# Sine in the place of the angles, a tile of its own for VectorE's turning from slab 4 on, and new numbers for the planned order

## The chip, the cores and the metric

The kernel runs on one core of a Trainium2 chip. The metric is device time in microseconds (us) of one execution. Names of engines: PE is TensorE (matmuls and transposes), VectorE and ScalarE are the two vector engines that work beside it, GpSimd does next to nothing here, and SP issues the DMAs. Each engine works through its own list of instructions in order; semaphores hold an instruction until what it reads is there.

## The reference

The kernel computes a linear attention with a complex decay, and after it a gated feed-forward network. Everything is 32-bit float at the edge, except the three weight matrices, whose 64-bit words the kernel turns into 32-bit floats itself.

```python
mag = np.sqrt(a_re * a_re + a_im * a_im)
scale = np.minimum(mag, 0.999) / (mag + 1e-06)
a_re_n, a_im_n = a_re * scale, a_im * scale
for t in range(S):                       # 768 steps; B=4, H=8, D=48
    new_re = ar * S_re - ai * S_im
    new_im = ar * S_im + ai * S_re
    kv = np.einsum('bhd,bhe->bhde', k[:, :, t], v[:, :, t])
    S_re, S_im = new_re + kv, new_im
    y[:, :, t] = np.einsum('bhd,bhde->bhe', q[:, :, t], S_re)
...
g = x @ w_gate                           # 3072 tokens, 384 -> 1536
silu = g * (1.0 / (1.0 + np.exp(-g)))
out = (silu * (x @ w_val)) @ w_out       # 1536 -> 384
```

## The kernel before, in words

**Slabs and groups.** The 4 x 768 time steps are cut into 24 slabs of 128 steps with all 8 heads, and two slabs (two batches, the same stretch of time) make a group; there are 12 groups, numbered 0 to 11. Within a slab the attention is a masked product of keys and queries, plus a state `G` that is handed from one stretch of time to the next. The complex decay is taken out beforehand: keys and queries are scaled by the exponentials of cumulated logarithms and turned by the cosine and sine of cumulated angles, which doubles their 48 columns per head to 96.

**Staging a group** (`stage_ops`, planned for two slabs at a time, for group 0 for one slab each). Loads of the decay's real and imaginary part (tiles `re` and `im`), their squares (L366), the logarithm, and by a triangular matmul (L438) its cumulated sum; two exponentials (L453, L454); products of keys and queries with them (`kt`, `qt`); the arc tangent of the ratio, written to `im`; its cumulated sum (L441); the sum is reduced to a fraction of a turn in the tile called `s` (slot `s3`). Of that fraction the last row is sent to DRAM (the step `fr`), since the next stretch of time adds to it. Then ScalarE takes the absolute value, the cosine into `u`, and the sine over the fraction itself, in `s`. That last write must wait until `fr` has read the row. Four products make `ks` and `qs` of these (the step `turn`: twice with `u`, twice with `s`). Many tiles share a place: slot `s3`, for instance, also holds the logarithm of the next group, and slot `im` the next group's loaded `im`, so a place that is held longer makes the next group's load or logarithm start later.

**A slab's attention** (`slab_ops`). Keys and queries are transposed to a tile `T` with the 96 columns on the partitions. There are two ways. For the first slabs (before: slabs 0 to 5) PE does it, in four batches of four 128 x 96 transposes (L565) into a bank `p_gv`, and ScalarE or VectorE copies each batch to `T`. For the others VectorE transposes blocks of 32 x 32 (L585, two instructions for a slab) into a tile that is free once the weights have been split (`spare("w")`, named `ww`), and 12 DMAs on SP's queue move the blocks to their places in `T`. Then come the scores (L614, PE), the mask (L620, VectorE), the output product `av` (L645, PE), its copy to `xh` (L654, ScalarE) and the rounding rest `xl` (L661, VectorE), and the state's product `kv` (L672, PE) with its additions to `G`.

**The network** (`ffn_ops`) takes a group's `xh` and `xl` in 12 steps (g,f), f from 0 to 11: `f1` (L825, 18 matmuls, 12 in group 0) into a bank `p_gv`, of which there are two; the silu (L831, ScalarE); the product (L836, VectorE); the rounding to `hh` and the rest `hl` (L291); `f2` (L859, 6 matmuls, 4 in group 0) into `p_po`. `f1` of a group begins when `xh` and `xl` of both of its slabs are there.

**Weights.** VectorE turns each block's 64-bit words into floats in three steps (L724, L728, L732), group 0 uses them whole, and afterwards each block is split into two rounded halves (a cast, then a subtraction) that all later groups use. `range_ops` reads each weight block once more by a DMA into a tile `wo` and tests its range with one VectorE (L777) and one ScalarE instruction (L782); these 36 tests lie in the stretch behind group 0.

**What sets the order.** A planner (class `Planner`) is given every step by name, with the engines that may run it and a cost for each, its dependencies, and the slots that it takes or uses. It hands out the steps one after the other by due time, and the instructions are then written to each engine's list in that order. Due times of the network and the attention come from the anchors `T0`, `PER`, `FT`, `FT0`, `LEAD0`, `LEAD2`, `AHEAD`; those of the weights from `CONV0`, `CONVP`; those of the tests from `CK0`, `CKP`; other steps take theirs from what follows them. Where two engines may do a step, the planner chooses. Where ScalarE needs another function table, an ACT_TABLE_LOAD (L942) stands in its list.

## Time and profile before

| what | us |
|---|---|
| median of 3 runs (lowest to highest) | 661.78 (660.48 to 664.44) |
| the profiled execution | 661.93 |
| its span, first to last instruction | 660.2 |
| PE busy / VectorE busy / ScalarE busy | 626.5 / 500.6 / 398.5 |

What is not in the span, 661.93 - 660.2 = 1.73 us, lies around it. The page gives each engine's busy time and, by line, what its instructions cost and what they waited for; a window counts what each engine did in a stretch of the span; a row of the timeline is one instruction or some alike: its start, its duration, and in square brackets how long the engine had stood idle and what ended that. Successive matmuls overlap, so what one costs on PE is read from one start to the next.

### The profile page before, as it was taken

What the parts mean: (1) busy time and instruction counts of PE and PEld (TensorE: products, weight loads), DVE (VectorE), ACT (ScalarE), POOL (GpSimd) and SP (SyncE); (2) the same over time, 40 slices, a digit from 0 to 9 for tenths busy, and PEclk for the clock granted to TensorE, in tenths of its full rate; (3) what the DMA queues carried; (4) which work ended last, traced back from release to release, by engine and by line L of the source; (5) the groups of instructions that cost most, each with busy time, mean ns of one, the idle gap of its engine ahead of it and who ended that gap; (6) DMA issues with size and microseconds to landing.
All of it is one profiled execution on the core that took longest, in us unless ns stands there. A gap on an engine that the chain in (4) does not pass through costs nothing.

```text
span 660.2 us, 15503 instructions
## 1 busy us (share of the span) xinstructions
PE 626.5 (95%) x6306; PEld 586.9 (89%) x6306; DVE 500.6 (76%) x923; ACT 398.5 (60%) x654; POOL 3.0 (0%) x9
## 2 busy tenths in 40 slices
PE   2689999999998999999999999999999999999996
PEld 0367778899998998999999999999999999999996
DVE  8799999989877876976976976967876966643332
ACT  7855259876875866756956766967846836311110
POOL 1000000000000000000000000000000000000000
PEclk9999999999999899999999999999999999999999
DMA  9999502346745646655755656655543530320000
GB/s 190 302 296 288 134 25 62 65 92 124 163 104 121 168 110 130 155 135 120 159 128 125 150 130 131 138 132 118 122 104 65 125 85 12 75 57 1 25 1 29
DMA packets 234932, 77.49 MB, mean 117 GB/s; under 512 B 208859, under 2 KB 230621, under 8 KB 234854
## 3 DMA queue, kind: packets, MB, share of 16 engines
q1 hardware_dynamic: 234854, 76.43, 48.8%
q8 instruction: 51, 0.84, 0.6%
q14 instruction: 27, 0.22, 0.1%
HBM read 57.47 MB, written 4.78 MB: 94 GB/s over the span
## 4 chain that ended last, share of the span: by engine, by line
PE 65%; DVE 18%; DMA 7%; ACT 6%; issue 3%; SPq 0%; ACTq 0%; DVEq 0%
PE p_gv L825 34%; PE p_po L859 17%; PE p_ps L614 5%; PE p_py L645 5%; ACT L942 2%; DVE xl L728 2%; ACT s L346 2%; PE p_pm L672 1%; PE p_pm L441 1%; DMA wo<-in_moe_w_val_dram 1%; DVE sg L836 1%; DMA kt<-in_k_dram 1%; DMA wo<-in_moe_w_gate_dram 1%; DVE s L291 1%; DVE ks L291 1%
## 5 line engine op out<-in xcount | busy, mean ns | idle before, releaser
L825 PE MATMUL p_gv<-xh,ww 128*128 128x256 f32 x1596 | 316.8, 294 | 1.2 <-DVE sg L836 1.1
L825 PEld LDWEIGHTS p_gv<-xh,ww 128*128 128x128 f32 x1596 | 260.0, 190 | 9.0 <-DVE sg L836 2.5
L825 PE MATMUL p_gv<-xl,ww 128*128 128x256 f32 x726 | 204.6, 282 | 0.0
L942 ACT ACT_TABLE_LOAD x111 | 142.4, 1283 | 2.0
L831 ACT ACTIVATE sg<-p_gv 128x256 f32<-128x256 f32 x144 | 54.2, 383 | 140.4 <-PE p_gv L825 139.6
L825 PEld LDWEIGHTS p_gv<-xl,ww 128*128 128x128 f32 x726 | 137.6, 190 | 0.2 <-issue 0.2
L859 PE MATMUL p_po<-wo,hh 128*128 128x384 f32 x484 | 126.7, 343 | 0.0
L836 DVE TENSOR_TENSOR sg<-sg,p_gv 128x256 f32<-128x256 f32 x144 | 58.6, 413 | 63.9 <-ACT sg L831 63.9
L859 PEld LDWEIGHTS p_po<-wo,hh 128*128 128x128 f32 x484 | 82.0, 189 | 2.3 <-issue 2.2
L859 PE MATMUL p_po<-wo,hl 128*128 128x384 f32 x242 | 81.4, 336 | 0.0
L291 DVE TENSOR_TENSOR hl<-sg,hh 128x256 fp32r<-128x256 f32 x132 | 54.3, 418 | 7.0 <-ACT hh L295 1.7
L614 PE MATMUL p_ps<-T 96*128 96x128 f32 x384 | 53.2, 279 | 0.0
L614 PEld LDWEIGHTS p_ps<-T 96*128 96x128 f32 x384 | 50.7, 196 | 0.9 <-ACT T L295 0.3
L859 PEld LDWEIGHTS p_po<-wo,hl 128*128 128x128 f32 x242 | 45.4, 188 | 0.0
L295 ACT CAST hh<-sg 128x256 fp32r<-128x256 f32 x49 | 19.7, 403 | 34.5 <-DVE sg L836 29.4
L346 ACT ACTIVATE s<-s 128x768 f32<-128x768 f32 x44 | 36.7, 842 | 4.0 <-DVE s L291 3.5
L645 PE MATMUL p_py<-sc,vt 128*32 128x128 f32 x768 | 37.1, 273 | 1.2 <-ACT xh L654 0.7
L777 DVE TENSOR_REDUCE flags<-wo 128x1 f32<-128x384 f32 x36 | 19.7, 547 | 24.4 <-DMA wo<-in_moe_w_val_dram 11.1
L620 DVE TENSOR_TENSOR sc<-p_ps,tri 128x512 f32<-128x512 f32 x48 | 32.8, 682 | 4.0 <-PE p_ps L614 3.4
L645 PE MATMUL p_py<-T,G 96*32 96x128 f32 x640 | 33.5, 280 | 0.0
L825 PE MATMUL p_gv<-xh,ww-1_412 128*128 128x256 f32 x132 | 27.4, 297 | 1.6 <-ACT xh L654 1.6
L782 ACT ACTIVATE wo<-wo 128x384 f32<-128x384 f32 x36 | 20.2, 561 | 12.3 <-DMA wo<-in_moe_w_gate_dram 5.4
(134 smaller groups left out, 804.5 us busy)
## 6 DMA issues: line engine op xcount, KB each, us to landing
T<-ww SPq DMA_DIRECT2D x216, 64.0 KB, 2.1
wo<-in_moe_w_out_dram SPq DMA_DIRECT2D x24, 384.0 KB, 5.6
ww<-in_moe_w_gate_dram SPq DMA_DIRECT2D x12, 384.0 KB, 5.1
vt<-in_v_dram SPq DMA_DIRECT2D x24, 192.0 KB, 4.0
ww<-in_moe_w_val_dram SPq DMA_DIRECT2D x12, 384.0 KB, 6.2
out_dram<-ost SPq DMA_DIRECT2D x24, 192.0 KB, 2.3
wo<-in_moe_w_gate_dram SPq DMA_DIRECT2D x12, 384.0 KB, 3.4
wo<-in_moe_w_val_dram SPq DMA_DIRECT2D x12, 384.0 KB, 4.0
```

The costliest lines, as they stand in the source:

```text
L291: V[e].tensor_tensor(out=out, in0=a, in1=b, op=op)
L295: nc.scalar.copy(out=out, in_=in_)
L346: nc.scalar.activation(out=of(dst), in_=of(source), func=func, scale=scale, **kw)
L614: nc.tensor.matmul(out=ps[:, hh, :], lhsT=kT(4 * qd + hh), rhs=qT(4 * qd + hh), start=True, stop=True)
L620: nc.vector.tensor_tensor(out=s, in0=at_["ps", f"{n}.{qd}"].rearrange("p (h t) -> p h t", h=4), in1=mask.unsqueeze(1).to_broadcast([P, 4, ...
L645: nc.tensor.matmul(out=o, lhsT=l, rhs=r, start=opens, stop=closes, tile_position=(0, 32 * slot))
L782: nc.scalar.activation(out=high(0), in_=high(1), func=AF.Square, accum_out=flags[:, fl_hi + j:fl_hi + j + 1])
L825: nc.tensor.matmul(out=gv[:, i, :], lhsT=l, rhs=r, start=(m == 0), stop=(m == len(mm) - 1))
L831: nc.scalar.activation(out=new("sg", I), in_=at_["gv", I][:, 0:2 * P], func=AF.Silu)
L836: nc.vector.tensor_tensor(out=sg, in0=sg, in1=at_["gv", I][:, 2 * P:4 * P], op=ALU.mult)
L859: nc.tensor.matmul(out=po, lhsT=l[:, cs], rhs=weight("o", f, part), start=f == 0 and j == 0, stop=f == NF - 1 and j == len(products) - 1)
L942: nc.scalar.preload_act_table_set(op.load)
```

## The change

Four things are edited. The sine is written to the place of `im`, which is no longer needed by then, instead of over the fraction; the dependency on `fr` is dropped, and `im` stays held until the products with the sine are made. The limit between the two ways of transposing goes from slab 6 to slab 4 (`TURN`). VectorE's way now has a tile of its own (`turned`, slot `bt`) instead of the spare weight tile, so that it no longer waits for the weights' split or for the end of group 0. To make room for that tile the scratch space for dynamic DMAs is set to 8192. And the costs, the anchors and other numbers that the planner goes by are replaced, which moves instructions everywhere.

```diff
--- before.py
+++ after.py
@@ -29,20 +29,20 @@
 INV_2PI = 0.15915494309189535
 LN999_2 = 2.0 * math.log(0.999)
 
-SWITCH = 1.527
-HOP = 0.189
-SWITCH_KEY = 8.8
-STRETCH = 1.749
-AHEAD, YIELD, QUEUED = -15.32, 14.38, 5.384
-T0, PER, FT, FT0 = 47.32, 23.02, 3.999, 5.679
-LEAD0, LEAD2 = 8.605, 2.123
-CONV0, CONVP = 39.06, 28.89
+SWITCH = 1.216
+HOP = 0.155
+SWITCH_KEY = 8.525
+STRETCH = 0.957
+AHEAD, YIELD, QUEUED = 14.73, 14.3, 3.586
+T0, PER, FT, FT0 = 50.04, 22.62, 3.712, 3.252
+LEAD0, LEAD2 = 13.23, 3.651
+CONV0, CONVP = 36.84, 13.29
 T1 = T0 + 12 * FT0
-CK0, CKP = 167.9, 18.96
-RCP, SQR = 1, 2
+CK0, CKP = 171.5, 11.84
+RCP, SQR, TURN = 1, 2, 4
 HIGH, LOW, WHOLE = 0, 1, 2
-SHY = -9.417
-POOL_FROM = 9.827
+SHY = -49.96
+POOL_FROM = -53.93
 
 
 
@@ -218,6 +218,8 @@
 
         return work.tile([P, 2 * WIDE[nm]], dtype, name=f"w{nm}{f}", tag=f"w{nm}{f}", bufs=1)
 
+    tile_t = const.tile([P, 4 * DM], F32, name="turned")
+
     def spare(nm):
 
         if nm not in W:
@@ -262,7 +264,7 @@
         for j in range(2):
             fixed["lent", t, j] = at[:, H * j:H * j + H], nm_f
     for i in range(2):
-        slots["ww", i] = slots["wo", i] = 1
+        slots["ww", i] = slots["wo", i] = slots["bt", i] = 1
     for t in fixed:
         slots[t] = 1
     pl = Planner(slots)
@@ -271,7 +273,7 @@
     def new(tag, inst):
         if tag in fixed:
             t = fixed[tag][0]
-        elif tag[0] in ("ww", "wo"):
+        elif tag[0] in ("ww", "wo", "bt"):
             t = None
         elif tag in PSUMS:
             t = psum.tile([P, 512], F32, name="p_" + tag, tag=tag, bufs=2 if tag == "po" else slots[tag])
@@ -520,9 +522,9 @@
             pl.add("fr" + N, {"SP": 0.55}, fr, deps=["frac" + N], use=[tg("s")], lat=2.0)
         act("abs", "u", "s", AF.Abs, None, ["frac"])
         act("cos", "u", "u", AF.Sin, "sin", ["abs"], scale=-TWO_PI, bias=b_half_pi)
-        act("sin", "s", "s", AF.Sin, "sin", ["abs", "fr"], scale=-TWO_PI)
+        act("sin", "im", "s", AF.Sin, "sin", ["abs"], scale=-TWO_PI)
         for dst, t in (("ks", "kt"), ("qs", "qt")):
-            for j, (cs, w) in enumerate(((slice(0, D), "u"), (slice(D, 96), "s"))):
+            for j, (cs, w) in enumerate(((slice(0, D), "u"), (slice(D, 96), "im"))):
                 opens = dst == "ks" and j == 0 and first == 0
                 after = [] if opens or dst == "qs" else [f"ks0_{g}a" if first else "ks0_" + N]
 
@@ -552,7 +554,7 @@
 
             return at_["T", n][:, x].rearrange("p (g i c m) -> p g i c m", g=4, i=4, m=2)
 
-        if n < 6:
+        if n < TURN:
             tdeps = []
             for i, st in ((1, "ks"), (0, "qs")):
                 for hq in range(2):
@@ -574,17 +576,16 @@
                     tdeps.append(pl.add("ev" + inst, {"ACT": 0.5, "DVE": 0.6}, ev, deps=["tr" + inst] + tdeps[:1],
                                         alloc=[] if tdeps else [("T", n)], use=[("gv", inst)] + ([("T", n)] if tdeps else [])))
         else:
-            halves = [(("ww", 0), f"b{n}"), (("ww", 1), f"b{n}")]
-            def bt():
-                return spare("w").rearrange("p (j x n) -> p j x n", j=3, x=2)
+            halves = [(("bt", 0), f"b{n}"), (("bt", 1), f"b{n}")]
+            bt = tile_t.rearrange("p (j x n) -> p j x n", j=3, x=2)
             for i, st in ((1, "ks"), (0, "qs")):
                 def tr(e, i=i, st=st):
                     if i == 1:
                         for t in halves:
                             new(*t)
-                    nc.vector.transpose(out=bt()[:, :, i].rearrange("p j (g c m) -> p g m j c", g=4, m=2),
+                    nc.vector.transpose(out=bt[:, :, i].rearrange("p j (g c m) -> p g m j c", g=4, m=2),
                                         in_=stack(st).rearrange("p (g m) (j c) -> p g m j c", j=3, m=2))
-                pl.add(f"tr{i}_{n}", {"DVE": 0.87}, tr, deps=made[st] + ([f"tr1_{n}"] if i == 0 else [f"c5{NF - 1}w", f"f1_0.{NF - 1}"]),
+                pl.add(f"tr{i}_{n}", {"DVE": 0.87}, tr, deps=made[st] + ([f"tr1_{n}"] if i == 0 else []),
                        alloc=halves if i == 1 else [], use=[stacks[st]] + (halves if i == 0 else []))
             for i in range(4):
                 def sh(e, i=i):
@@ -592,7 +593,7 @@
                         new("T", n)
                     for j in range(3):
                         nc.sync.dma_start(out=at_["T", n][32 * j:32 * j + 32].rearrange("p x (g i n) -> p (x g) i n", g=4, i=4)[:, :, i],
-                                          in_=bt()[32 * i:32 * i + 32, j].rearrange("p x (g n) -> p (x g) n", g=4))
+                                          in_=bt[32 * i:32 * i + 32, j].rearrange("p x (g n) -> p (x g) n", g=4))
                 pl.add(f"sh{i}_{n}", {"SP": 1.65}, sh, deps=[f"tr0_{n}"] + ([f"sh0_{n}"] if i else []),
                        alloc=[] if i else [("T", n)], use=halves + ([("T", n)] if i else []), lat=1.3, move=0.5)
             tdeps = [f"sh{i}_{n}" for i in range(4)]
@@ -612,7 +613,7 @@
                 ps = new("ps", f"{n}.{qd}").rearrange("p (h t) -> p h t", h=4)
                 for hh in range(4):
                     nc.tensor.matmul(out=ps[:, hh, :], lhsT=kT(4 * qd + hh), rhs=qT(4 * qd + hh), start=True, stop=True)
-            pl.add(f"sc{qd}_{n}", {"PE": 0.88}, sc, deps=tdeps + [f"sc0_{n}" if qd else f"sc1_{n - 1}"],
+            pl.add(f"sc{qd}_{n}", {"PE": 0.86}, sc, deps=tdeps + [f"sc0_{n}" if qd else f"sc1_{n - 1}"],
                    alloc=[("ps", f"{n}.{qd}")], use=[("T", n)], key=ta + qd)
 
             def mk(e, qd=qd):
@@ -643,7 +644,7 @@
             for step in zip(*turns):
                 for slot, (o, l, r, opens, closes) in enumerate(step):
                     nc.tensor.matmul(out=o, lhsT=l, rhs=r, start=opens, stop=closes, tile_position=(0, 32 * slot))
-        pl.add("av" + N, {"PE": 2.2 if c else 1.3}, av, deps=[f"mk0_{n}", f"mk1_{n}", "ldv" + N, f"gm{n - 4}"],
+        pl.add("av" + N, {"PE": 2.1 if c else 1.4}, av, deps=[f"mk0_{n}", f"mk1_{n}", "ldv" + N, f"gm{n - 4}"],
                alloc=[("py", n)], use=[("sc", f"{n}.0"), ("sc", f"{n}.1"), ("T", n), ("vt", n)], key=ta + 5)
 
         cols = slice(half * P, half * P + P)
@@ -671,7 +672,7 @@
                     for j in range(3):
                         nc.tensor.matmul(out=pk[32 * j:32 * j + 32, h, :], lhsT=ks[:, h, 32 * j:32 * j + 32],
                                          rhs=vt[:, h, 0:D], start=True, stop=True, tile_position=(0, 32 * j))
-            pl.add("kv" + N, {"PE": 1.1}, kv, deps=made["ks"] + ["ldv" + N, "av" + N], alloc=[("pm", "K" + N)],
+            pl.add("kv" + N, {"PE": 0.82}, kv, deps=made["ks"] + ["ldv" + N, "av" + N], alloc=[("pm", "K" + N)],
                    use=[("ks", ("ks", g)), ("vt", n)], key=ta + 5.1)
             gv, dec = G[:, b, :, 0:D], lambda: at_["dec", g][:, hs].unsqueeze(2).to_broadcast([96, H, D])
 
@@ -823,7 +824,7 @@
                         mm += [(wh[:, kt, :], xh[:, kt, :])] if g == 0 else [(wh[:, kt, :], xh[:, kt, :]), (wh[:, kt, :], xl[:, kt, :]), (wl[:, kt, :], xh[:, kt, :])]
                     for m, (l, r) in enumerate(mm):
                         nc.tensor.matmul(out=gv[:, i, :], lhsT=l, rhs=r, start=(m == 0), stop=(m == len(mm) - 1))
-            pl.add("f1_" + I, {"PE": 2.16 if g else 2.6}, f1,
+            pl.add("f1_" + I, {"PE": 2.15 if g else 2.6}, f1,
                    deps=[f"ev{'l' if g else 'h'}{2 * g + i}" for i in range(2)] + [f"c{5 if g else 3}{f}w", f"f1_{g}.{f - 1}", f"f1_{g - 1}.{NF - 1}"],
                    alloc=[("gv", I)], use=[("xh", g), ("xl", g)] if g else [("xh", g)], key=key)
 
@@ -859,7 +860,7 @@
                         nc.tensor.matmul(out=po, lhsT=l[:, cs], rhs=weight("o", f, part),
                                          start=f == 0 and j == 0, stop=f == NF - 1 and j == len(products) - 1)
             PO = [("po", g)]
-            pl.add("f2_" + I, {"PE": 1.06 if g else 1.31}, f2,
+            pl.add("f2_" + I, {"PE": 1.05 if g else 1.31}, f2,
                    deps=([f"hl_{I}", f"c5{f}o"] if g else [f"h2_{I}", f"c3{f}o"]) + ([f"f2_{g}.{f - 1}"] if f else []),
                    alloc=PO if f == 0 else [], use=([("hh", I), ("hl", I)] if g else [("sg", I)]) + (PO if f else []), key=key + 3)
         for i in range(2):
@@ -1088,7 +1089,7 @@
     from concourse import mybir as _mybir
     from concourse.bass_utils import run_bass_kernel_spmd as _run
 
-    nc = _bacc.Bacc("TRN2", target_bir_lowering=False, num_devices=1)
+    nc = _bacc.Bacc("TRN2", target_bir_lowering=False, num_devices=1, dynamic_dma_scratch_size=8192)
     arrays, args = {}, []
     for name in _INS:
         a = _np.ascontiguousarray(inputs[name])
```

Counted over the two lists, PE has 32 transposes fewer (16 each of slabs 4 and 5), VectorE 4 block transposes more (L586 in the changed kernel, where all lines stand one or two lower), SP 24 transfers to `T` more, and ScalarE 17 table loads more (128, 111 before). VectorE makes 4 copies of `T` fewer and ScalarE 4 fewer; 11 casts in staging and 7 of `hh` go from VectorE to ScalarE, and 4 copies of the output from ScalarE to VectorE.

Three places show how the order changes.

**Slab 4.** Before, PE's list has the sixteen transposes of slab 4 between `f2` of step (1,4) and `f1` of step (1,6) (L565; `ident` is the unit matrix, `ww_933` the weights of that step). In the changed kernel VectorE's list has the two block transposes of that slab ahead of a product of group 1.

Before, PE:

```order
L859 MATMUL p_po<-wo_959,hh 128x384 x2
L859 MATMUL p_po<-wo_959,hl 128x384
L859 MATMUL p_po<-wo_959,hh 128x384 x2
L859 MATMUL p_po<-wo_959,hl 128x384
L565 MATMUL p_gv<-ident,ks 96x128 x8
L565 MATMUL p_gv<-ident,qs 96x128 x8
L825 MATMUL p_gv<-xh,ww_933 128x256
L825 MATMUL p_gv<-xl,ww_933 128x256
```

Changed, VectorE:

```order
L662 TENSOR_TENSOR xl<-p_py,xh 128x3x128
L293 TENSOR_TENSOR ks<-kt,s_860 128x16x48
L293 TENSOR_TENSOR G<-p_pm,dec 96x8x48
L293 TENSOR_TENSOR ks<-kt,im 128x16x48
L293 TENSOR_TENSOR wo_940<-wo_214,wo_940 128x384
L586 STREAM_TRANSPOSE turned<-ks 128x4x2x3x32
L293 TENSOR_TENSOR re<-re,s_886 128x768
L586 STREAM_TRANSPOSE turned<-qs 128x4x2x3x32
L837 TENSOR_TENSOR sg<-sg,p_gv 128x256
```

The transposes are gone from between two steps on PE; on VectorE the turned keys and queries are transposed directly behind their last factors, with a step of group 3's staging (`re`) between the two.

**Slab 7's copy to `xh`.** On ScalarE before, the last instruction ahead of the cast to `xh` is the range test of a weight block (L782, reading the tile `wo_1396`), and ahead of the first silu of group 3 there is nothing but two steps of staging.

Before, ScalarE:

```order
L831 ACTIVATE sg<-p_gv 128x256
L346 ACTIVATE s_2297<-s_2297,b_half_pi 128x768
L782 ACTIVATE wo_1396,flags<-wo_1396 128x384
L654 CAST xh<-p_py 128x3x128
L346 ACTIVATE s_1968<-s_1968 128x768
L366 ACTIVATE s_2413<-re 128x768
L831 ACTIVATE sg<-p_gv 128x256
```

Changed, ScalarE:

```order
L783 ACTIVATE wo_1717,flags<-wo_1717 128x384
L943 ACT_TABLE_LOAD
L832 ACTIVATE sg<-p_gv 128x256
L655 CAST xh<-p_py 128x3x128
L783 ACTIVATE wo_1717,flags<-wo_1717 128x384
L832 ACTIVATE sg<-p_gv 128x256
L348 ACTIVATE s_2214<-s_1757 128x768
L297 CAST hh<-sg 128x256
L348 ACTIVATE s_2214<-s_2214,b_half_pi 128x768
L348 ACTIVATE im<-s_1757 128x768
```

The cast (L655 in the changed kernel) now stands directly behind a silu of group 2, and the next range test behind it; four more silus of group 2, (2,8) to (2,11), stand between it and the first of group 3, where before there was none.

**The end.** Behind the last `f1`, (11,11), PE's list had `f2` of three steps before and has it of two now.

Before, PE:

```order
L825 MATMUL p_gv<-xh,ww_1198 128x256
L859 MATMUL p_po<-wo_1183,hh 128x384 x2
L859 MATMUL p_po<-wo_1183,hl 128x384
L859 MATMUL p_po<-wo_1183,hh 128x384 x2
L859 MATMUL p_po<-wo_1183,hl 128x384
L892 MATMUL p_pm<-ones,good 1x1
L859 MATMUL p_po<-wo_1223,hh 128x384 x2
L859 MATMUL p_po<-wo_1223,hl 128x384
L859 MATMUL p_po<-wo_1223,hh 128x384 x2
L859 MATMUL p_po<-wo_1223,hl 128x384
L859 MATMUL p_po<-wo_1299,hh 128x384 x2
L859 MATMUL p_po<-wo_1299,hl 128x384
```

Changed, PE:

```order
L826 MATMUL p_gv<-xh,ww_1568 128x256
L860 MATMUL p_po<-wo_1570,hh 128x384 x2
L860 MATMUL p_po<-wo_1570,hl 128x384
L860 MATMUL p_po<-wo_1570,hh 128x384 x2
L860 MATMUL p_po<-wo_1570,hl 128x384
L860 MATMUL p_po<-wo_1608,hh 128x384 x2
L860 MATMUL p_po<-wo_1608,hl 128x384
L860 MATMUL p_po<-wo_1608,hh 128x384 x2
L860 MATMUL p_po<-wo_1608,hl 128x384
```

Of the rows behind `f1` those of step (11,9) and the verdict's sum (L892) are gone from this place; they stand ahead of it now.

## The prediction

> **What bounds the kernel now.** I read the page's first lines, then the windows by stage, then the timeline wherever PE stands idle in them.
>
> ```profile
> span 660.2 us, 15503 instructions
> PE 626.5 (95%) x6306; PEld 586.9 (89%) x6306; DVE 500.6 (76%) x923; ACT 398.5 (60%) x654; POOL 3.0 (0%) x9
> ...
> 0.00:44.00 44.00, 25.25 (x241) 16.03 (x241) 37.49 (x62) 34.77 (x58) 2.95 (x9) 1.00 0.99 261
> 44.00:105.00 61.00, 58.16 (x413) 45.94 (x413) 61.00 (x106) 27.80 (x41) 0.00 (x0) 1.00 0.53 149
> 105.00:160.00 55.00, 53.57 (x536) 50.55 (x535) 51.87 (x90) 44.11 (x70) 0.00 (x0) 1.00 0.45 91
> 160.00:220.00 60.00, 57.26 (x634) 55.16 (x633) 48.53 (x90) 41.63 (x70) 0.00 (x0) 0.97 0.59 132
> 220.00:660.00 440.00, 432.28 (x4490) 419.21 (x4489) 301.66 (x579) 250.23 (x417) 0.00 (x0) 1.00 0.43 100
> ```
>
> The columns of a window are its length, the busy time of PE, of its weight loads, of VectorE, ScalarE and GpSimd, then the granted clock, the DMAs' share and their rate. PE sets the end. It idles 18.75 us of the first 44, until there is something to multiply, and behind that only 2.84, 1.43, 2.74 and 7.72 us in the four windows; of the last, 660.2 - 654.35 = 5.9 us lie behind the last matmul (its row stands below), where only copies and a store run. So beside PE's own work there are some nine microseconds to win behind 44. VectorE is full in 44:105, 61.00 of 61 us, and 94% busy in the next window: what is put on it there can come back as a wait of PE. The sum goes against the profiled execution's 661.93 us, which is the median of 661.78 and 0.15.
>
> **Transposes off PE: -3.5.**
>
> ```profile
> 78.52 0.60 PE L565 MATMUL p_gv<-ident,ks 128*96 128x128 f32 x4
> 78.96 0.60 PE L565 MATMUL p_gv<-ident,qs 128*96 128x128 f32 x4
> ```
>
> Four transposes take 78.96 - 78.52 = 0.44 us of PE, start to start. Slabs 4 and 5 lose eight such batches: 8 x 0.44 = 3.5. PE is back to back there, so this counts in full as long as nothing else becomes late.
>
> **The waits around slab 4: -2.1.**
>
> ```profile
> 128.36 0.60 PE L565 MATMUL p_gv<-ident,ks 128*96 128x128 f32 x4
> ...
> 130.61 0.64 PE L565 MATMUL p_gv<-ident,qs 128*96 128x128 f32 x4 [0.83 <-DVE T L297]
> ...
> 132.27 0.38 PE L825 MATMUL p_gv<-xh,ww 128*128 128x256 f32 x1
> ...
> L585 DVE STREAM_TRANSPOSE ww<-ks 128x768 f32<-128x768 f32 x18 | 17.5, 973 | 3.5 <-DMA T<-ww 2.9 <-issue 0.6
> ...
> T<-ww SPq DMA_DIRECT2D x216, 64.0 KB, 2.1
> ```
>
> The batches share the two `p_gv` banks with `f1`, so each waits for a copy or a product, as the row at 130.61 shows. From 128.36 to 132.27 are 3.91 us, of which 4 x 0.44 = 1.8 is work; the other 2.1 vanish with it. In their place slab 4's scores need two block transposes and 12 DMAs, which land 2.1 us after their issue (last column). Queued behind these on SP are group 3's loads, at a DMA share of 0.45 in that window. The new order leaves at least one `f1` between the transposes and the scores, so I put this at nothing; uncovered it costs some 2 us for each of the two slabs. VectorE gains 4 x 0.97 of transposes and loses four copies, and that goes into its own term below.
>
> The Trainium skill speaks against this step: "VectorE: DVE Perf Modes", section "Rules for kernel authors", advises TensorE for a 128 x 128 transpose if PSUM will do as its destination. By that rule these two terms would be nothing and the sum 5.6 us higher; the windows above, where PE is the full engine from 105 on, speak against the rule here.
>
> **The stall ahead of group 3: -4.2.**
>
> ```profile
> 210.95 0.88 PE L672 MATMUL p_pm<-vt,ks 128*32 128x48 f32 x48
> 213.45 0.38 PE L825 MATMUL p_gv<-xh,ww-1_412 128*128 128x256 f32 x1 [1.61 <-ACT xh L654]
> ...
> 218.19 0.63 PE L859 MATMUL p_po<-wo,hh 128*128 128x384 f32 x2
> ...
> 212.39 0.55 ACT L782 ACTIVATE wo<-wo 128x384 f32<-128x384 f32 x1 [2.26 <-DMA wo<-in_moe_w_out_dram]
> ...
> 212.93 0.46 ACT L654 CAST xh<-p_py 128x384 fp32r<-128x384 f32 x1
> ...
> 216.00:218.00 2.00, 2.00 (x12) 2.00 (x11) 2.00 (x4) 0.84 (x1) 0.00 (x0) 0.50 0.90 180
> ...
> DVE flags L777 <- DMA wo<-in_moe_w_val_dram: 11.1, 5, 4.1
> ...
> 648.81 0.40 PE L825 MATMUL p_gv<-xh,ww 128*128 128x256 f32 x2
> ...
> 649.17 0.40 PE L825 MATMUL p_gv<-xh,ww 128*128 128x256 f32 x2
> ```
>
> `av` stands ahead of `kv`, so its result was there by 211; but in ScalarE's list the cast to `xh` stands behind a range test that waits for its weights until 212.39. The first step of group 3 starts late, and then runs at a granted clock of 0.50: from the end of `kv`, 211.83, to the next `f2`, 218.19, pass 6.36 us. At full clock three matmuls of `f1` take 649.17 - 648.81 = 0.36, 18 of them 2.15; so the stall and the slow clock behind it cost 6.36 - 2.15 = 4.2. In the new order that cast stands four steps ahead of its use. A step is 2.15 for `f1` and, with six matmuls half as long again, 1.07 for `f2`: 4 x 3.2 = 12.8 us of PE's work, against a longest wait of a test for its weights of 4.1 us (total, times, longest in the row of L777). Late next would be the casts ahead of groups 4 to 11; their lead in the new order is as long. The bounds are 0, if the stall only moves, and -4.2.
>
> **The start: -0.9.**
>
> ```profile
> 23.51 0.52 ACT L346 ACTIVATE ww<-ww 128x384 f32<-128x384 f32 x1 [1.82 <-DMA fr<-ww]
> 41.71 0.68 DVE L620 TENSOR_TENSOR sc<-p_ps,tri 128x512 f32<-128x512 f32 x1
> 43.90 2.87 PE L825 MATMUL p_gv<-xh,ww 128*128 128x256 f32 x12
> 47.59 0.64 PE L565 MATMUL p_gv<-ident,ks 128*96 128x128 f32 x4 [0.82 <-DVE ks L291]
> 48.94 0.64 PE L565 MATMUL p_gv<-ident,ks 128*96 128x128 f32 x4 [0.71 <-ACT T L295]
> ```
>
> The sine no longer waits for `fr`, 1.82 us at 23.51. But that is on ScalarE, while the last mask of slab 1 (41.71), on which the first `f1` (43.90) hangs, stands in VectorE's list, and VectorE was busy 37.49 of the first 44 us. Walked through the new order with the durations of before, that mask ends 0.9 earlier; the two waits behind `f1` (0.82 and 0.71) go, and other work takes their place. I take -0.9; the bounds are 0 and -0.9 - 1.5 = -2.4.
>
> **VectorE between 44 and 160: +1.8.**
>
> ```profile
> 38.04 0.95 DVE L728 SCALAR_TENSOR_TENSOR xl<-ww,xl 128x768 uint32<-128x768 uint32 x1
> 38.91 0.95 DVE L291 TENSOR_TENSOR qt<-qt,qs 128x768 f32<-128x768 f32 x1
> ...
> 103.78 1.62 PE L859 MATMUL p_po<-wo,sg 128*128 128x384 f32 x4 [1.31 <-DVE sg L836]
> ...
> 105.38 0.42 DVE L836 TENSOR_TENSOR sg<-sg,p_gv 128x256 f32<-128x256 f32 x1
> ```
>
> One 768-wide instruction takes 38.91 - 38.04 = 0.87 start to start. Ahead of the last product of group 0 (105.38 to 105.8) the new list has 9.5 us more of group 2's staging and 8.0 less of weight splits: 1.5 more. Its start, walked through as above, leaves VectorE 2.8 us less idle, so that product ends near 105.8 + 1.5 - 2.8 = 104.5. PE's own work up to the `f2` that needs it adds up to 75.1 us in the new order; with the 27.2 that it has lost by the first `f1` (43.90 less 16.7 of work) and 0.6 of small waits it could start there at 102.9. The wait is 1.6, in place of today's 1.31 at 103.78: +0.3. By the product of (1,6) VectorE has 9.8 us more ahead of it than before (four transposes, 3.9, and group 3's staging), by (2,0) again 0.7 less; the two `p_gv` banks take up most of this, and I take +1.5. Together +1.8. The bounds are 0 and +6, the 9.8 less the 3.9 that come from PE.
>
> **The end: +0.7.**
>
> ```profile
> 650.91 0.39 ACT L831 ACTIVATE sg<-p_gv 128x256 f32<-128x256 f32 x1 [2.79 <-PE p_gv L825]
> ...
> 652.18 0.43 DVE L291 TENSOR_TENSOR hl<-sg,hh 128x256 fp32r<-128x256 f32 x1
> ...
> 654.01 0.34 PE L859 MATMUL p_po<-wo,hl 128*128 128x384 f32 x1
> ```
>
> Between the last `f1` and its `f2` lie 1.7 us of silu, product and rounding (650.91 to 652.61). Two `f2` cover them now; in the new order one does, 1.07 long, and 0.6 to 0.7 stays open.
>
> **Table loads and small waits: +1.**
>
> ```profile
> 57.45 1.28 ACT L942 ACT_TABLE_LOAD   x1
> 58.74 0.84 ACT L346 ACTIVATE s<-re 128x768 f32<-128x768 f32 x1
> ```
>
> 17 more loads of 1.28 are 21.8 us on ScalarE, and 18 casts come to it beside; it is busy 60% of the span, and at the most 44.11 of 55 us in a window behind 44, so most of this hides behind PE. Where a load stands ahead of a silu, the `f1` two steps on waits for the bank. Between nothing and 17 x 0.25 = 4 us I take 1, near the end that the idle time speaks for. The Trainium skill, "ScalarE: Activation LUTs", section "What ACT_TABLE_LOAD costs", gives 1.28 us for a load and 1.38 more for draining. These rows agree on the load; they show no drain, as the next instruction starts when it ends. By the page the loads would be an estimated 45 us of ScalarE's time.
>
> **The sum.** 661.93 - 3.5 - 2.1 - 4.2 - 0.9 + 1.8 + 0.7 + 1 = 654.7; against the median 654.6.
>
> **Rivals.** *More is won* (chance 0.17): VectorE's term and the small waits are nothing and the start gives its -2.4: 654.6 - 2.8 - 1.5 = 650.3. For it speaks the longer lead of the casts in all groups; against it, that PE idles only 7.72 - 5.9 = 1.8 us between 220 and its last matmul. *No gain* (0.16): VectorE pays the transposes back at its bound, 6 in place of 1.8, and the test's wait meets another cast, +4.2 less what is covered: 658.8 to 663. For it: 61.00 of 61 us; against it: by (2,0) VectorE's list is shorter than before. *Slower* (0.12): the sine keeps the place `im` until both products with it are made, and the next group's load waits for that.
>
> ```profile
> im<-in_a_im_dram SPq DMA_DIRECT2D x11, 384.0 KB, 4.9
> ```
>
> From that load (4.9) to the products the chain has some five passes on ScalarE (0.84), three table loads (1.28) and ten passes on VectorE (0.87): 21.6 us, with PE's sums and the hand-overs an estimated 28. A group lasts (654.35 - 220) / 9 = 48, so 20 are spare. If the queues on ScalarE and VectorE eat those 20, the loop becomes the period, and each microsecond beyond counts nine times: 1 us takes all the gain, 2 us give 654.6 + 18 = 673. For it: eight of the 17 loads come ahead of group 1. Against it: VectorE is 69% and ScalarE 57% busy behind 220. That the change does not do what it says is met by the order, in which the transposes are gone.
>
> **Chances.** The forecast's own case, 651 to 658.5, has 0.55, and 0.17 + 0.55 = 0.72 is faster by over 0.5% (under 658.5; 0.5% is about what a measurement of this kernel can tell from no change). Within 0.5% is 0.16, slower 0.12. The range, 648 to 662, holds the first three cases but for the far ends, and leaves out the slow one.
>
> **What would show it.** Right: no L826 row that waits for `xh` between 200 and 215 and a clock of 1.00 there; nothing on PE where slab 4's and 5's transposes stood; the last matmul near 647. Wrong: waits of L826 or L860 for the product (L837) between 100 and 160 that add up to over 3 us; waits of the scores (L615) for `T`; loads of `im` that ScalarE or VectorE waits for in every group; new waits for `xh` behind 220.

## The result: slower by 1.5%, and where the time went

| | median us | runs | lowest to highest | ratio to before, 95% interval |
|---|---|---|---|---|
| before | 660.53 | 5 | 659.68 to 664.44 | |
| changed | 671.50 | 5 | 671.37 to 672.59 | 1.0153, 1.0121 to 1.0185 |

I forecast 654.6, with a range of 648 to 662, and measured 671.5. The changed kernel's first lines and its chain, from its page:

```profile
span 669.7 us, 15372 instructions
PE 623.9 (93%) x6274; PEld 583.0 (87%) x6274; DVE 497.9 (74%) x907; ACT 428.4 (64%) x683; POOL 3.0 (0%) x9
...
PE 42%; ACT 20%; DVE 18%; DMA 7%; SPq 7%; issue 6%; DVEq 0%; ACTq 0%
...
L615 PE MATMUL p_ps<-T 96*128 96x128 f32 x384 | 54.3, 283 | 5.2 <-DMA T<-turned 3.8
...
L783 ACT ACTIVATE wo<-wo 128x384 f32<-128x384 f32 x36 | 20.2, 560 | 29.1 <-DMA wo<-in_moe_w_val_dram 12.7
```

PE has 2.6 us less to do, as it should, and yet the span is 9.5 longer. PE's share of the chain fell from 65% to 42%; ScalarE's rose from 6% to 20%, and SP's queue, which was at 0%, has 7%. The range test on ScalarE (L783) now stands behind 29.1 us of idle time; its group on the page of before showed 12.3. PE's waits answer to the same, from the list of waits (total, times, longest):

```profile
PE p_pm L443 <- DVE s L504: 4.2, 4, 1.5
PE p_ps L615 <- DMA T<-turned: 3.8, 2, 3.3
...
PE p_gv L826 <- DVE sg L837: 3.2, 10, 0.8
PE p_gv L826 <- ACT xh L655: 3.2, 1, 3.2
```

In the kernel before the first was 0.5 us in all and the second did not occur. To see where the time was lost I set the starts of the same step side by side (first matmul of `f1` in the two timelines):

| step | before | changed | difference |
|---|---|---|---|
| (0,0) | 43.9 | 50.5 | +6.6 |
| (0,2) | 54.2 | 59.7 | +5.5 |
| (2,0) | 160.5 | 163.9 | +3.4 |
| (3,4) | 228.9 | 232.2 | +3.2 |
| (7,0) | 418.8 | 426.2 | +7.4 |
| (11,0) | 613.4 | 623.5 | +10.0 |
| end of the last matmul | 654.3 | 663.2 | +8.8 |

There are two losses: 6.6 us before there is any network step, and 7 us strewn over groups 3 to 10. Between them, to (3,4), the change wins a little, but far less than the 8 us that the prediction's terms put there (-3.5 - 2.1 - 4.2 + 1.8). The start, on VectorE, ScalarE and SP and then on PE:

```profile
45.04 0.68 DVE L621 TENSOR_TENSOR sc<-p_ps,tri 128x512 f32<-128x512 f32 x1
...
44.95 0.82 ACT L348 ACTIVATE im<-s 128x768 f32<-128x768 f32 x1
45.80 1.28 ACT L943 ACT_TABLE_LOAD   x1
49.23 0.84 ACT L348 ACTIVATE s<-re 128x768 f32<-128x768 f32 x1 [2.15 <-issue]
49.98 0.46 ACT L655 COPY xh<-p_py 128x384 f32<-128x384 f32 x1
...
44.72 0.34 SPq L521 DMA_DIRECT2D fr<-s  x1
...
46.38 0.92 PE L673 MATMUL p_pm<-vt,ks 128*32 128x48 f32 x42
50.49 7.14 PE L826 MATMUL p_gv<-xh,ww 128*128 128x256 f32 x24 [3.19 <-ACT xh L655]
```

The sine (44.95) indeed no longer waits for `fr`. Behind it in ScalarE's list stands the logarithm of the next group, which writes the place `s` that `fr` reads. `fr` is issued at 44.72, at a DMA share of 0.99 from there to 49.2, and the logarithm starts 4.5 us later. The copy to `xh`, for which PE waits 3.19 us, stands behind that logarithm. This is one half of the first loss. The other half was there before it: the last mask of slab 1 starts at 45.04, where it started at 41.71 before, so it is 3.3 us late. PE's first transposes are already that late (28.28, and 24.77 before). ScalarE, which is busy without a break at that time, makes the first exponentials of group 0 at 16.53 in place of 13.50. Which of the changed numbers put them there was not tested.

### The profile page after: what moved, and what is told of

Same layout as the page of the kernel before. It is cut to its first block, busy times and chain, and to the rows that moved or that the text cites. A ratio compares the mean times of both kernels' runs of the same rounds, so it can differ in the third digit from the quotient of the medians.

```text
span 669.7 us, 15372 instructions
## 1 busy us (share of the span) xinstructions
PE 623.9 (93%) x6274; PEld 583.0 (87%) x6274; DVE 497.9 (74%) x907; ACT 428.4 (64%) x683; POOL 3.0 (0%) x9
## 4 chain that ended last, share of the span: by engine, by line
PE 42%; ACT 20%; DVE 18%; DMA 7%; SPq 7%; issue 6%; DVEq 0%; ACTq 0%
PE p_gv L826 22%; PE p_po L860 11%; ACT L943 10%; SPq L595 5%; ACT s L348 4%; PE p_ps L615 3%; PE p_py L646 3%; DVE s L293 2%; DVE sg L837 2%; ACT sg L832 2%; DMA fr<-s 2%; DMA wo<-in_moe_w_out_dram 1%; ACT im L348 1%; DVE turned L586 1%; PE p_pm L443 1%
## 5 line engine op out<-in xcount | busy, mean ns | idle before, releaser
L826 PE MATMUL p_gv<-xh,ww 128*128 128x256 f32 x1596 | 313.0, 292 | 6.7 <-DVE sg L837 3.2
L615 PEld LDWEIGHTS p_ps<-T 96*128 96x128 f32 x384 | 51.3, 199 | 7.5 <-issue 5.9
L297 ACT CAST hh<-sg 128x256 fp32r<-128x256 f32 x56 | 22.6, 403 | 25.4 <-DVE sg L837 24.2
L783 ACT ACTIVATE wo<-wo 128x384 f32<-128x384 f32 x36 | 20.2, 560 | 29.1 <-DMA wo<-in_moe_w_val_dram 12.7
L348 ACT ACTIVATE s<-s 128x768 f32<-128x768 f32 x33 | 27.9, 846 | 6.4 <-DVE s L293 6.0
L646 PEld LDWEIGHTS p_py<-sc,vt 128*32 128x32 f32 x768 | 23.5, 109 | 2.6 <-DVE sc L621 1.6
```

The lines of the kernel that those rows point to most:

```text
L297: nc.scalar.copy(out=out, in_=in_)
L348: nc.scalar.activation(out=of(dst), in_=of(source), func=func, scale=scale, **kw)
L615: nc.tensor.matmul(out=ps[:, hh, :], lhsT=kT(4 * qd + hh), rhs=qT(4 * qd + hh), start=True, stop=True)
L646: nc.tensor.matmul(out=o, lhsT=l, rhs=r, start=opens, stop=closes, tile_position=(0, 32 * slot))
L826: nc.tensor.matmul(out=gv[:, i, :], lhsT=l, rhs=r, start=(m == 0), stop=(m == len(mm) - 1))
```

## The experiments

Ratios are to the kernel before on the same chip. "Order kept" means that the order of the steps was written down and not planned again. The changed kernel's 671.50 was measured beside a before of 660.53; where a run is set against it below, counting each from its own before makes the gain 0.3 to 0.9 us smaller (best_new 1.4).

| run | median us | before's median | ratio, 95% interval |
|---|---|---|---|
| sine_only | 668.72 | 660.20 | 1.0124, 1.0086 to 1.0162 |
| turn_only | 665.23 | 660.20 | 1.0079, 1.0059 to 1.0099 |
| edits_old_numbers | 673.23 | 660.20 | 1.0210, 1.0191 to 1.0230 |
| turn_in_old_order | 674.17 | 659.70 | 1.0226, 1.0190 to 1.0262 |
| log_behind_copy | 665.67 | 660.20 | 1.0077, 1.0051 to 1.0104 |
| after_warm | 666.38 | 659.70 | 1.0104, 1.0075 to 1.0133 |
| after_no_tests | 661.99 | 659.70 | 1.0024, 1.0004 to 1.0044 |
| before_no_tests | 654.01 | 659.70 | 0.9920, 0.9894 to 0.9946 |
| test_behind_copy | 658.47 | 659.14 | 0.9981, 0.9965 to 0.9998 |
| tests_three_places | 656.48 | 659.14 | 0.9952, 0.9934 to 0.9970 |
| best_new | 659.80 | 659.14 | 0.9999, 0.9980 to 1.0017 |
| two_mends | 661.86 | 659.64 | 1.0027, 1.0014 to 1.0041 |

### Are the edits slow, or the new numbers?

Three kernels with the planner's numbers of before: all edits, the sine alone, the turning alone. Each is planned again. edits_old_numbers, against the changed kernel:

```diff
-AHEAD, YIELD, QUEUED = 14.73, 14.3, 3.586
-T0, PER, FT, FT0 = 50.04, 22.62, 3.712, 3.252
+AHEAD, YIELD, QUEUED = -15.32, 14.38, 5.384
+T0, PER, FT, FT0 = 47.32, 23.02, 3.999, 5.679
...
```

sine_only and turn_only, against the kernel before:

```diff
-        act("sin", "s", "s", AF.Sin, "sin", ["abs", "fr"], scale=-TWO_PI)
+        act("sin", "im", "s", AF.Sin, "sin", ["abs"], scale=-TWO_PI)
...
```

```diff
-RCP, SQR = 1, 2
+RCP, SQR, TURN = 1, 2, 4
...
-        if n < 6:
+        if n < TURN:
...
```

> The three edits (sine to the place of im, turning on VectorE from slab 4, tile of its own), planned with the numbers of before. If the loss lies in the replaced numbers, the edits keep what they take off PE (-3.5 of transposes, -2.1 of waits): 653 to 658 us. If the edits themselves cost the time (the place im held longer, the logarithm behind fr, more DMAs on SP), it is slower than before: 664 to 672.

> Before, with the sine alone written to the place of im. If that only moves the wait for fr from the sine to the next logarithm, 659 to 663 (no change). If the held place lengthens the loop of staging, 665 to 675, with loads of im that land later in every group.

> Before, with VectorE turning from slab 4 on in a tile of its own, and nothing else. By the sum of the prediction 661 - 5.6 + 0 to 2: 655 to 658. If VectorE's full stretch pays it back, 660 to 663.

Measured 673.2, 668.7 and 665.2: each is slower, and the edits with the old numbers are not faster than with the new ones (671.5). So the edited kernel is slow with either set of numbers; the new numbers without the edits were not tried. But a planner gives every edit a new order throughout, so this says little about the edits themselves. In sine_only, for instance, PE waits 2.45 us at 63 for a product whose silu stands behind a square that waits 4.09 us for its load of `re`; that is a place in that order and not a cost of the sine. What the sine alone costs in an unchanged order was not tried: there, from group 2 on, the next group's load into `im` stands ahead of the sine.

### The turning alone, in the order of before

Order kept; only slabs 4 and 5 are changed. In the list of steps (P is PE, V VectorE, A ScalarE, S SP; `trt` and `evt` are the transposes on PE and their copies, `tr` the block transposes, `sh` three DMAs each), at the place of the first transpose, for slab 4 and alike for slab 5:

```diff
-trt410 P; trt411 P; evt410 V; trt400 P; evt411 V; evt400 V; trt401 P; evt401 A
+tr1_4 V; tr0_4 V; sh0_4 S; sh1_4 S; sh2_4 S; sh3_4 S
```

> The order of before kept as it is, step by step; only the sixteen PE transposes and eight copies each of slabs 4 and 5 are replaced by two block transposes and twelve DMAs, in the tile of its own, at the place where the first transpose stood. By the prediction's two terms 660.2 - 3.5 - 2.1 = 654.6. If VectorE, or the DMAs behind which the scores then wait, pays it back, 658 to 662. That turn_only was slower by 5 would then be the new order and not the edit.

Measured 674.2: slower by 14.5, where the prediction's two terms gave 5.6 less. PE and SP in its timeline:

```profile
140.55 2.05 PE L615 MATMUL p_ps<-T 96*128 96x128 f32 x8 [9.78 <-DMA T<-turned]
...
162.70 2.05 PE L615 MATMUL p_ps<-T 96*128 96x128 f32 x8 [5.68 <-DMA T<-turned]
...
129.66 0.95 DVE L586 STREAM_TRANSPOSE turned<-qs 128x768 f32<-128x768 f32 x1
...
130.63 7.90 SPq L595 DMA_DIRECT2D T<-turned  x12
```

The scores wait 9.78 and 5.68 us for `T`, and behind both waits the granted clock reads 0.50 (138 to 142 and 164 to 168), so that PE loses more than the waits. The twelve DMAs do land 2.1 us after their issue, but issuing them takes 7.90 us, 0.66 each, one behind the other on SP's queue: from the last block transpose at 130.6 to the scores at 140.55 are 10 us. I had taken the 2.1 alone as the price. The trace of before held the right one, in slabs that were turned that way already (SP's timeline):

```profile
191.43 6.97 SPq L594 DMA_DIRECT2D T<-ww  x9
```

Nine in 6.97. In this run the DMAs stand where PE's transposes stood, so almost nothing covers them. The changed order starts the staging of slabs 4 and 5 earlier, and there they cost PE little: the scores of slab 4 do not wait at all, those of slab 5 wait 0.6 us (146.88). The two waits for `T` in the changed kernel are of other slabs, 7 (3.25 us at 196.26) and 16 (0.53 at 440), which VectorE turned in both kernels. For slab 7 SP's list shows why:

```profile
182.05 1.91 SPq L595 DMA_DIRECT2D T<-turned  x3
184.05 1.50 SPq L797 DMA_DIRECT2D wo<-in_a_re_dram  x1
185.65 1.29 SPq L797 DMA_DIRECT2D ww<-in_a_im_dram  x1
187.00 7.46 SPq L595 DMA_DIRECT2D T<-turned  x9
```

Two loads of another test (L797, a check of the decay's values) now stand among slab 7's twelve DMAs, so that these take 12.4 us to issue (182.05 to 194.46); before, one load of a weight stood among them, and they took 9.6 (188.84 to 198.40).

### The logarithm behind `fr`

The changed kernel's order with one step moved.

```diff
+    order.remove(at["lnr2"])
+    order.insert(order.index(at["evh1"]) + 1, at["lnr2"])
...
```

> The changed kernel's order with one step moved: group 2's logarithm of re goes behind slab 1's copy to xh on ScalarE. The logarithm writes the place that the transfer fr of group 1 still reads, and the copy stood behind it. If that wait makes the first f1 late, f1 starts near 47.3 in place of 50.5 and the end comes 3 us earlier, 668 to 669. If weights or VectorE are what f1 (0,1) and later wait for, the end moves by less than 1 us: 670.5 to 672.

Measured 665.7, 5.8 less than the changed kernel, twice what I expected. ScalarE and PE:

```profile
44.78 0.48 ACT L655 COPY xh<-p_py 128x384 f32<-128x384 f32 x1 [0.90 <-PE p_py L646]
45.27 1.28 ACT L959 ACT_TABLE_LOAD   x1
47.27 0.84 ACT L348 ACTIVATE s<-re 128x768 f32<-128x768 f32 x1 [0.71 <-issue]
...
45.33 5.45 PE L826 MATMUL p_gv<-xh,ww 128*128 128x256 f32 x24
```

The copy runs as soon as its product is there, and `f1` starts at 45.33. The first two steps then take 5.45 us where they took 7.14: in the changed kernel PE's wait was followed by a slow stretch (granted clock 0.50 in 52 to 54), so a wait of 3.2 cost nearly 5. The whole gain is 5.2 us at the first step and stays to the end (last matmul 658.0 for 663.2). Not all of it is the moved step: in this execution the matmuls also became fast earlier (next section), and the last mask came at 43.14 in place of 45.04. In two_mends, which has the same move without that luck, the first `f1` starts at 47.0, a gain of 3.5. That this step is what PE waited for is shown. That the logarithm waits for `fr` is shown too. The views name no releaser ("issue"), but the trace holds the semaphores: the last update of the one that tells of `fr`'s landing comes at 49.16 in the changed kernel, 4.4 us after the issue, ScalarE's wait for that semaphore ends at 49.18, and the logarithm starts at 49.23. The same three times follow one another in this kernel (47.20, 47.22, 47.27), in two_mends (48.34, 48.37, 48.41) and in after_no_tests below (48.73, 48.76, 48.80, and PE waits 4.95).

### Was it the slow clock at the start?

In the changed kernel eight transposes at 28.28 take 1.91 us, and 1.04 at 39.15; in the kernel before they are at the shorter time from 31.25 on. I put matmuls without use into PE's gaps, which is this loop and a step made of it.

```diff
+            for _ in range(times):
+                nc.tensor.matmul(out=t[:, 0:P], lhsT=tri, rhs=tri, start=True, stop=True)
...
```

> The changed kernel's order with 34 matmuls without use (unit triangle by itself, into a bank that is free then) put on PE between its first sums, 14 behind the sum that starts at 21.3 and 20 behind the one at 24.1, so that PE is not idle in 22 to 28. If PE's slow matmuls until 37.5 come from its being idle so much before, they are fast some 5 us earlier, the first mask too, and the end comes 1 to 3 us earlier: 668.5 to 670.5. If the half speed has another cause, or is not on the path, 671 to 673.

Measured 666.4, 5.1 less, but not for the reason given. From best_new, which has the same matmuls (timeline, then windows):

```profile
21.81 3.65 PE L967 MATMUL p_ps<-tri 128*128 128x128 f32 x14
25.26 1.59 PE L440 MATMUL p_pm<-im,tri 128*128 128x384 f32 x2
26.08 4.93 PE L967 MATMUL p_ps<-tri 128*128 128x128 f32 x20
30.81 1.91 PE L567 MATMUL p_gv<-ident,ks 128*96 128x128 f32 x8
32.51 1.34 PE L440 MATMUL p_pm<-s,tri 128*128 128x384 f32 x2
33.69 1.04 PE L567 MATMUL p_gv<-ident,ww 128*96 128x128 f32 x8
...
24.00:28.00 4.00, 4.00 (x16) 3.39 (x16) 4.00 (x7) 3.97 (x8) 0.00 (x0) 1.00 1.03 207
```

PE is busy without a gap from 21 to 32, and still eight transposes take 1.91 at 30.81; they are fast from 33.7 on here and, by the same reading, from 36 on in after_warm. My expectation that idle time keeps it slow fell. Two kernels with the same start, log_behind_copy and two_mends, become fast at 33.7 and at 37.5, which goes with a first `f1` at 45.3 and at 47.0; so it varies from one execution to the next. The gain of after_warm lies elsewhere: the wait for the copy is 1.46 in place of 3.19 and the wait for `T` at 190 is 1.82 in place of 3.25, since other things met. Its profiled execution (663.42) is also one of the two shortest of its seven, so the trace shows more gain than the median has. Why the useless matmuls help there stays open.

### The range tests

Left out of both kernels, each in its own order: these two kernels do not test the weights' range; the flags are set to a passing value.

```diff
+    order = [op for op in order if not (op.name[:2] in ("kl", "k1", "k2") and op.name[2:].isdigit())]
...
```

> The changed kernel's order with the 36 range tests of the weights left out (their transfers, VectorE's and ScalarE's instruction; their flags are set to a passing value). If the tests' waits for weights, ahead of the angle sums on VectorE and ahead of silus on ScalarE, are what makes each group from 4 on longer, the 6 us that the changed kernel loses between groups 4 and 11 mostly go: 662 to 666. If the table loads or the held place of the sine make the groups longer, 669 to 671.

> The kernel before, in its own order, with the 36 range tests left out in the same way. By the prediction's term the stall ahead of group 3 goes with its slow clock: -4.2, so 656. If something else ends that wait next, 658 to 660.

Measured 662.0, 9.5 less than the changed kernel (8.7 counted from its own before), and 654.0, 5.7 less than before. So in the changed kernel the tests cost 3 to 4 us more. The rest of its loss is not the tests: without them in either, on one chip, the changed order is still 8.0 us slower. The two traces show 5.2 us of that at (0,0), 3.5 at (2,0) and 8.0 at (3,4), and between the last two PE waits 3.1 for slab 7's `T`. What they do there, VectorE and then PE in the changed kernel's timeline:

```profile
403.93 0.55 DVE L778 TENSOR_REDUCE flags<-wo 128x1 f32<-128x384 f32 x1 [4.19 <-DMA wo<-in_moe_w_gate_dram]
404.40 0.68 DVE L621 TENSOR_TENSOR sc<-p_ps,tri 128x512 f32<-128x512 f32 x1
...
410.38 0.55 DVE L778 TENSOR_REDUCE flags<-wo 128x1 f32<-128x384 f32 x1
410.87 0.95 DVE L386 TENSOR_REDUCE flags<-re 128x1 f32<-128x768 f32 x1
411.74 0.41 DVE L837 TENSOR_TENSOR sg<-sg,p_gv 128x256 f32<-128x256 f32 x1
412.07 0.55 DVE L504 SCALAR_TENSOR_TENSOR s<-p_pm,s 128x384 f32<-128x384 f32 x1
...
412.68 0.62 PE L443 MATMUL p_pm<-s,tri 128*128 128x384 f32 x2 [1.51 <-DVE s L504]
```

A test waits 4.19 us for its weights, and the masks, products and angle sums behind it in VectorE's list are late; the next one, with no wait of its own, still stands ahead of the sum (412.07) that empties the one bank `p_pm`, and PE waits 1.51 us for that bank. Groups 5 to 8 have the same order and PE the same wait, 0.45 to 1.51. Without the tests PE's waits for L504 are gone from the list, and the step (7,0) comes 8.8 us earlier, (3,4) only 0.1. So the growth from group 3 to 8 is the tests. Another 2.5 us between (9,0) and (11,0) stay without them. There PE waits 0.79 and 0.37 us for products of VectorE (at 529.79 and 534.67), which it does not before, and ten more matmuls (917 for 907) fall into that stretch, which the kernel before does later.

Groups 4 to 8 take (526.7 - 270.1) / 5 = 51.3 us each in the changed kernel and 50.6 before; without the tests 49.9 and 50.1. So the loop through the place `im`, my rival for slower, is not what sets the period. Nor does any instruction of the changed kernel wait for a load of `im`; in the kernel before three waited, 3.1 us in all.

### One test behind the copy, in the kernel before

```diff
+    for name, behind in (("k25", "evh7"), ("k15", "evl7"), ("kl6", "k15")):
+        order.remove(at[name])
+        order.insert(order.index(at[behind]) + 1, at[name])
...
```

> The kernel before in its own order, with the one range test that stood ahead of slab 7's copy put behind it, on ScalarE and on VectorE (and the next test's load behind that). By the prediction's term the stall at 211 and the slow clock behind it go, -4.2: 655.5 to 656.5. If the next test or the next load takes its place, 658.5 to 660.5.

```profile
208.97 0.48 ACT L654 CAST xh<-p_py 128x384 fp32r<-128x384 f32 x1
211.35 0.56 ACT L782 ACTIVATE wo<-wo 128x384 f32<-128x384 f32 x1 [1.90 <-DMA wo<-in_moe_w_out_dram]
...
210.07 0.88 PE L672 MATMUL p_pm<-vt,ks 128*32 128x48 f32 x48
210.88 0.38 PE L825 MATMUL p_gv<-xh,ww-1_412 128*128 128x256 f32 x1
```

The cast no longer stands behind the test, and `f1` of group 3 follows `kv` without a gap. Yet the median is 658.5 for 659.1, 0.2% faster, where the last matmuls of the two profiled executions are 3.5 us apart. The profiled execution of before, 661.93, was one of its longer ones (the 22 runs that stand beside this one: 658.4 to 662.5, median 659.1). A stall with a slow clock behind it that is worth 4.2 us in one execution is worth 0.7 in the median. Only that one execution has a trace, so what the others do at 211 is not shown.

### Three places for the tests, and three mends of the changed kernel

tests_three_places keeps the order of before and turns slabs from 6 on as before, but in a tile of its own; the weight tile that this sets free gives the tests two more places, so that each load is issued two tests earlier. best_new is the changed kernel with that, the logarithm moved and the matmuls without use; two_mends is best_new without these matmuls.

```diff
+            def home(j=j):
+                return spare("w")[:, 2 * DM * (j % 3 - 1):2 * DM * (j % 3)] if j % 3 else spare("o")
...
+    slot = {max(1, j - 2): [] for j in range(1, 3 * NF)}
+    for j in range(1, 3 * NF):
+        slot[max(1, j - 2)].append(loads[j])
...
```

> The order of before, slabs turned from 6 on as before but in the tile of its own, and the weight tile that this sets free used for the range tests: they read from three places in turn, so each load is issued two tests earlier than before. If the tests cost what they do (5.7 us without them) because each waits for its weights, most of that comes back: 654.5 to 656.5. If it is the work and the transfers of the tests themselves, 658.5 to 660.5.

> The changed kernel's order with three things mended: group 2's logarithm behind slab 1's copy, 34 matmuls without use ahead of 28 us, and the range tests in three places. If the three costs are separate, 671.5 - 5.8 - 2 to 5 - 6 to 9 = 652 to 658, faster than before. If the first two buy the same microseconds and the tests stay, 662 to 666.

> As the kernel with three mends, without the matmuls without use: the logarithm behind the copy and the tests in three places. If the late full clock and the logarithm's wait cost separately, this is 2 to 5 slower than with all three: 662 to 665. If they are the same microseconds, so that either mend alone buys them, 659 to 661.

Measured 656.5, 659.8 and 661.9. tests_three_places is faster than both kernels, 0.5% under before; it brings back 2.7 us of the 5.7 that the tests cost. No test waits for its weights any more (before, VectorE's stood 24.4 us idle ahead of them and ScalarE's 12.3), so the other 3 us are not these waits; whether they are the tests' work or their transfers was not tested. Nor was the turning tile's own place tested apart from the two places that it sets free. The changed kernel's loss is undone by its mends: two bring 9.6 of the 11 us, all three make it equal to before. But before had no mend; against tests_three_places, which has the same places for its tests, best_new is still 3.3 us slower. They are not separate costs that add up (5.8, 5.1 and up to 9.5 alone). What the changed kernel has for itself, 3.5 us of transposes, shows in none of the medians: a wait for `T` remains (2.16 us at 190 in best_new), and the first `f1` starts 3.1 us later than before.

## Why the prediction was wrong, by its steps

- **Transposes off PE, -3.5.** Right on PE's own work (2.6 us less busy).
- **The waits around slab 4, -2.1.** They are gone, and in the changed order slabs 4 and 5 cost PE only 0.6 us of new waits, near the nothing that I put. But the price that I gave for the DMAs uncovered, "some 2 us for each of the two slabs", is wrong: it is 9.8 and 5.7 us, and a slow clock behind, since the issue of twelve DMAs itself takes 7.9. The new order then met this price at slab 7, 3.25 us, which no term had.
- **The stall ahead of group 3, -4.2.** The mechanism was right in both kernels: in the changed one no `f1` waits for `xh` at that place and the clock reads 1.00 from 200 to 220. The size was that of one execution: moving the test alone is worth 0.7 us in the median. And the same tests stall VectorE, and through it PE, at other places in the new order. The bound "0, if the stall only moves" was too kind: the tests cost 5.7 us before and 8.7 to 9.5 now.
- **The start, -0.9, bounds 0 and -2.4.** This step failed most: +6.6. It failed twice. The mask that I walked to, 0.9 us earlier by my count, came 3.3 later. And I left out the copy to `xh` behind it on ScalarE: I saw that the sine loses its wait for `fr` without asking who writes that place next. The row of before that shows the wait (1.82 at 23.51) told that `fr` can land late at the start; the logarithm took the wait over, ahead of an instruction that PE needs, and that cost 3.2 more.
- **VectorE between 44 and 160, +1.8.** Its waits did not come: between (0,2) and (2,0) PE waits 0.8 us for products of VectorE, less than the 1.3 and 0.2 before. That the stretch still gains only 2.1 us (5.5 to 3.4) is not explained in full. Some of it is order: six transposes of group 1 and slab 5's `kv` (0.9 us) lie in this stretch in the changed kernel only.
- **The end, +0.7.** PE waits 0.20 for the rounding at 661.75, so the size was less.
- **Table loads and small waits, +1, bounds 0 and 4.** Too small, if the tests' waits at new places are counted here: 3 to 4 us more than before. The 17 loads stand in the chain (L943 has 10% of it, 2% before) but were not tested apart.
- **The signs.** The three signs of a right forecast that concern steps came true or nearly so: no wait for `xh` between 200 and 215, the clock at 1.00 there, no transposes of slabs 4 and 5 on PE. The fourth, the last matmul near 647, did not (663.2). Of the signs of a wrong one only the waits of the scores for `T` showed (3.8 us, at other slabs); products (0.8 us between 100 and 160), loads of `im` and new waits for `xh` behind 220 did not. None of the signs watched the start, where the largest part was lost.
- **Rivals.** Slower had 0.12. That its number, 673, is close is luck: its mechanism is not the one, since the place `im` does not set the period.

## What to carry to other kernels

When an edit removes a wait for a transfer, look for the next instruction that writes the place the transfer reads, and for what stands behind that instruction in its engine's list. A load that an engine waits for in order delays everything behind it, so tests and other side work want their data landed before their turn comes; two more places for the tests' data, with the turning in a tile of its own, were worth 0.5% here, with no work removed. The price of a way through many DMAs is their count times the issue time, read off the queue's timeline, plus one landing.

## What was not expected of the hardware

PE's transposes ran at half their later speed for the first 31 to 38 us of the span, in best_new after PE had been busy for 10 us without a gap, and when they became fast differed by 3.8 us between two kernels with the same start. In best_new the column of the granted clock reads 1.00 in that stretch, but the trace's first record of the clock begins at 33.6, just ahead of the first fast transposes (33.69); a 1.00 ahead of that record shows nothing, and the durations decide. In the changed kernel, whose records begin at 20.7, the column reads 0.50 from 28 to 36, as the durations say. The Trainium skill, "TensorE: Matmul & The Clock Gate", section "What's actually happening", gives some 3.4 us of activity as the time after which matmuls are fast. The stretch of 21 to 32 in best_new does not agree: there it took over 12 us.

A PE wait of 3.19 us ahead of 50.49 was followed by a granted clock of 0.50 in 52 to 54, so that it cost 1.7 us more than itself (7.14 for 5.45 in the next two steps). And how long a small transfer takes depended on what else moved: the 3 KB row `fr` landed 4.4 us after its issue at 44.72, at a DMA share of 0.99, and 1.2 us after its issue at 101.83, at a share of 0.01.
